# An attention-and-experts kernel: VectorE's transposes moved to the front of a unit, a shorter routing tail, other loads for two units, and steps of the seam moved

## The chip, the core and the metric

The kernel runs on one core of a Trainium2 chip. A core has five engines with instruction streams of their own: TensorE (PE in the rows, with its weight loads as PEld), VectorE (DVE), ScalarE (ACT), GpSimd (POOL) and SyncE (SP, which only starts DMAs here). Each engine works through its stream in order and waits on semaphores for the others. The metric is the device time of one execution in microseconds; lower is better.

## The reference

Two stages. First, attention for 4 batches of 12 heads, 448 positions, head size 64: scores are q times k over 8, softly capped as cap * tanh(scores / cap), then a softmax, then the product with v. Second, the result, seen as 1792 rows of 768, goes to a mixture of 8 experts: each row takes the expert with the greatest gate logit, and its output is `gate probability * sigmoid(output-gate logit of that expert) * (relu(x @ w1[e]) @ w2[e])`. All is float32.

```
scores = cap * tanh((q @ k.T / 8) / cap);  attn = softmax(scores);  x = attn @ v
e = argmax(x @ w_gate);  p = softmax(x @ w_gate)[e];  s = sigmoid(x @ w_output_gate)[e]
out = p * s * (relu(x @ w1[e]) @ w2[e])
```

## The kernel before

**Attention in 24 units.** A unit is a pair of heads of one batch (6 units to a batch). The loop `for u in range(NU)` (L958) writes each engine's stream by hand, and that order is final. In unit u, `qk(u, s)` (L353) makes four score tiles s = 0 to 3 on TensorE, and ScalarE takes the tanh of each (L371); `expo(u)` (L374) is one exponential over the unit; `pv(u - 1, c)` (L382) multiplies the unit before by V while that goes on; `u_evac(u - 1)` (L400) copies that product out of PSUM, on VectorE up to unit 7 and again for units 21 and 22, else on ScalarE. `presum` (L385) adds up the exponentials on GpSimd (on VectorE for the last units), and `sums` (L408) finishes the softmax denominators on TensorE. The exponentials of a unit lie in one of two buffers, so a unit's tanh may not write until `presum` of the unit two before has read that buffer.

**K and Q.** For float32 precision each K and Q is held as a rounded high plane and a low plane. Unit 0 is loaded in rows (`load_first`, L110) and transposed by TensorE (`prep_first`, L341). All other units are loaded by `load_pair` (L116) in pieces of 32 floats and transposed by VectorE: `t_k(u)` and `t_q(u)` (L307, L310) run a transpose into the PSUM tile `tk` (L286), a copy to the high plane (L276) and a subtraction to the low plane (L282). These turns wait in a list; `turn_next(n)` (L326) takes the next n of it, `before` of them right after the unit's score matmuls and `after` of them behind the matmuls with V. The pair is (1, 1) unless the table `TURN` says otherwise. There are five buffers of K and Q planes, and turns run up to some three units ahead.

**The ring of score tiles.** `scores()` and `half()` (L334, L338) hand out three PSUM tiles in turn: to the score tiles, to the product with V, and to every small step of the router. A tile is given again three requests later, and TensorE waits until its last reader is done with it.

**The router, in slots.** When a batch's units are done, `end_of_batch(b)` (L443) has its steps carried out in slots of the next batch's units: "f", "g" ahead of `expo`, "h" behind it, "q" behind the matmuls with V, "e" at the end. The dictionary `at` says which step goes where, counted from the first unit after the batch. The steps: `gate_mm` and `gate_out` (gate logits of four or two units in a score tile, copied out by VectorE as `gsb`), `sums_out`, `sums_tr`, `recips`, `gate_tr` and `gate_mul`, `logits`, `choose` (argmax), `rank_mm`, `place`, `place2` (each row's place in its expert's list), `enter` (the table entry: row number and weight), `scatter` (entries to the tables in DRAM, by GpSimd). `row_tr` and `row_out` write the attention rows to `xs` in DRAM; `store_rows` issues those stores on SP's queue.

**The seam.** During units 20 to 23 `early()` plans the first five blocks of rows in six pieces (`nx`); `set_known` opens the loads, `fetch_dma(i)` reads a block's table (SP), `gather(i)` its rows (POOL), `load_raw` brings the weights of the first expert (`lds`, 14 pieces, SP). Then the experts' matmuls begin: `split_to` (L1033) makes high and low planes of each weight piece (ScalarE L1044, VectorE L1045), `tx` transposes rows, and `mm_chunk` multiplies (L1066). The last batch's router runs in between, as steps of `bg`.

Of the kernel before, what the change touches and what calls it, by code (L numbers as in the profile page):

```python
# [22 lines left out]
def tile_kernel(ctx: ExitStack, tc, q, k, v, cap, w_gate, w_ogate, w1, w2, out):  # L23
# [35 lines left out]
    TURN = {5: (1, 2), 6: (1, 2), 8: (1, 2), 10: (2, 2), 14: (1, 2), 15: (1, 2), 16: (1, 2)}  # L59
# [40 lines left out]
    k0 = raw2[0][:, 0:SK + 128].rearrange("p (c j d) -> p c j d", j=2, d=D)  # L100
    q0 = raw2[1][0:CP, 0:NCH * 2 * D].rearrange("p (c j d) -> p c j d", j=2, d=D)
# [8 lines left out]
    def load_first():  # L110
        k_, q_ = heads(k, 0), heads(q, 0)
        load_natural(k0, k_, NK, 128, (nc.sync, nc.scalar))
        nc.scalar.dma_start(out=k0[0:64, NK], in_=k_[:, SK:S].rearrange("j p d -> p j d"))
        load_natural(q0, q_, NCH, CP, (nc.sync, nc.scalar))
# [38 lines left out]
    load_first()  # L153
# [36 lines left out]
    load_k(1)  # L190
    load_q(1)
# [35 lines left out]
    ids = rtp.tile([CP, B, NCH], F32, name="ids")  # L227
    nc.gpsimd.iota(ids, pattern=[[S, B], [CP, NCH]], base=-NT, channel_multiplier=1,
# [60 lines left out]
    def q_planes(u, ps):  # L289
        hi, lo = part_tile("QH", [128, S]), part_tile("QL", [128, S])  # L290
        copy(u == 0, hi, ps)
        minus(lo, ps, hi)
        return [hi, lo]

    def k_planes(u, ps):
        hi, lo = kpl[u % PB]
        parts = [(hi[:, 0:SK], lo[:, 0:SK], ps[:, 0:SK])]
        for j in range(2):
            h, c = slice(64 * j, 64 * j + 64), slice(SK + 64 * j, SK + 64 * j + 64)
            parts.append((hi[h, c], lo[h, c], ps[h, SK:S]))  # L300
        for x, _, y in parts:
            copy(u == 0, x, y)
        for x, z, y in parts:
            minus(z, y, x)
        return [hi, lo]

    def t_k(u):  # L307
        pl[u] = k_planes(u, turned(ldk.pop(u), S))

    def t_q(u):  # L310
        pl[u] += q_planes(u, turned(ldq.pop(u), S))

    loads = [f for u in range(2, NU, 2) for f in ((load_k, u), (load_q, u))]
    tdone = {t_k: 0, t_q: 0}

    def load_ahead():
        while loads:
            f, u = loads[0]
            if u > tdone[t_k if f is load_k else t_q] + 5:
# [4 lines left out]
    turns = [f for u in range(1, NU) for f in ((t_k, u), (t_q, u))]  # L324
# [16 lines left out]
    def prep_first():  # L341
        pk = tbank([128, S], "tk0")
        for c in range(NK + 1):
            n = min(128, S - c * 128)
            nc.tensor.transpose(pk[:, c * 128:c * 128 + n], k0[0:n, c].rearrange("p j d -> p (j d)"), ident[0:n, 0:n])
        pq = scores("tq0")[:, 0, 0:S]
        for c in range(NCH):
            nc.tensor.transpose(pq[:, c * CP:(c + 1) * CP], q0[:, c].rearrange("p j d -> p (j d)"), ident[0:CP, 0:CP])
# [994 lines left out]
```

## Time and profile before

| | us |
|---|---|
| median of 3 runs (537.25 to 537.8) | 537.76 |
| profiled execution, its own time | 541.76 |
| span in that profile | 540.2 |
| tanh of the first unit starts | 8.66 |
| exponentials of the last unit start | 217.27 |
| first expert matmul | 230.49 |
| mean granted clock of TensorE | 0.976 |

TensorE is busy for 498.9 us of the span (92%), VectorE 391.0 (72%), ScalarE 369.0 (68%), GpSimd 289.4 (54%). Attention takes the first 217 us or so, and the experts the rest. Times in rows are microseconds from the span's start; a share of busy time mixes the two stages, so each stage has to be read by itself.

### The profile page before, as it was taken

Reading aid. Unit: us, or ns where it says so; the run is one execution under the profiler, and the core shown is the slowest. Engines: PE = TensorE matmul, PEld = TensorE weight load, DVE = VectorE, ACT = ScalarE, POOL = GpSimd, SP = SyncE. Lnnn points to the kernel's source line nnn. Section 1 sums busy time; section 2 is a strip of 40 time slices with the busy share of each in tenths; the row PEclk is TensorE's granted clock in tenths of the full one; section 3 lists DMA queues with packets and bytes.
Section 4 is the critical chain, followed back from the end, with each engine's and each line's share of the span. In section 5 each row is a group of like instructions: output and inputs, shape, how many; then the busy total and the mean of one; then the engine's idle time right before and its main releaser. Section 6 shows DMA issues by size and latency. Waiting matters only on the chain. (4 is left out here: it accounts for less than half of the span.)

```text
span 540.2 us, 10059 instructions
## 1 busy us (share of the span) xinstructions
PE 498.9 (92%) x3077; PEld 345.0 (64%) x3077; DVE 391.0 (72%) x713; ACT 369.0 (68%) x427; POOL 289.4 (54%) x360
## 2 busy tenths in 40 slices
PE   7699989959994989899999999999999999999994
PEld 5344355424452445267898997897879877666691
DVE  4578789987998666379898996894757685546450
ACT  5789877838874576554758896885766786555551
POOL 8999887776887530335625877214647035262001
PEclk9999999979998899989999999999999999999999
DMA  7978755843522043798319924419939969993001
GB/s 128 179 147 144 124 98 96 154 85 70 101 55 51 18 78 60 248 343 246 116 42 388 361 69 147 183 42 366 364 109 370 333 201 385 335 353 137 0 32 47
DMA packets 155932, 91.93 MB, mean 170 GB/s; under 512 B 138578, under 2 KB 138714, under 8 KB 155872
## 3 DMA queue, kind: packets, MB, share of 16 engines
q1 hardware_dynamic: 144000, 57.78, 40.6%
q0 software_dynamic: 8832, 32.74, 16.6%
q10 hardware_dynamic: 3040, 0.71, 0.6%
q8 instruction: 26, 0.43, 0.3%
q14 instruction: 34, 0.28, 0.2%
HBM read 123.68 MB, written 12.04 MB: 251 GB/s over the span
## 5 line engine op out<-in xcount | busy, mean ns | idle before, releaser
L1045 DVE TENSOR_TENSOR wr<-raw,wr 128x768 fp32r<-128x768 f32 (+1 forms) x167 | 172.1, 1067 | 70.6 <-ACT wr L1044 62.2
L1044 ACT ACTIVATE wr<-raw 128x768 fp32r<-128x768 f32 (+1 forms) x167 | 150.2, 935 | 38.4 <-DMA raw<-in_moe_w_dram 17.9
L371 ACT ACTIVATE pt<-s,icap 128x896 f32<-128x896 f32 x96 | 80.8, 914 | 40.8 <-PE s L364 28.0
L382 PE MATMUL u<-pt,vv 128*64 128x448 f32 x384 | 80.5, 563 | 1.3 <-ACT pt L371 0.8
L1066 PE MATMUL py<-wr,hh 128*128 128x384 f32 x352 | 77.3, 340 | 0.0
L1066 PE MATMUL php<-wr,xh 128*128 128x512 f32 x264 | 75.6, 408 | 0.0
L1135 POOL DMA_INDIRECT out_dram<-yo,ti x13 | 20.5, 1575 | 94.8 <-ACT yo L1133 70.6
L374 ACT ACTIVATE pt<-pt,capc 128x3136 f32<-128x3136 f32 x24 | 69.9, 2912 | 0.6
L1066 PEld LDWEIGHTS py<-wr,hh 128*128 128x128 f32 x352 | 61.2, 188 | 4.0 <-issue 3.7
L393 POOL TENSOR_TENSOR pa<-pt 128x896 f32<-128x896 f32 x20 | 42.1, 2106 | 25.9 <-ACT pt L374 19.4
L1066 PEld LDWEIGHTS php<-wr,xh 128*128 128x128 f32 x264 | 48.0, 190 | 12.2 <-issue 1.8
L382 PEld LDWEIGHTS u<-pt,vv 128*64 128x64 f32 x384 | 26.3, 142 | 43.5 <-issue 36.5
L398 POOL TENSOR_TENSOR pb<-pb,pt 64x448 f32<-64x448 f32 x40 | 45.6, 1141 | 3.1
L1066 PE MATMUL py<-wr,hl 128*128 128x384 f32 x176 | 44.8, 335 | 0.0
L394 POOL TENSOR_TENSOR pb<-pa,pt 128x896 f32<-128x896 f32 x20 | 42.2, 2111 | 1.6
L1066 PE MATMUL php<-wr,xl 128*128 128x512 f32 x132 | 41.9, 398 | 0.0
L1182 POOL DMA_DIRECT2D rh<-in_moe_w_dram x42 | 23.2, 556 | 21.9 <-DVE wr L1045 13.6
L286 DVE STREAM_TRANSPOSE tk<-raw 128x448 f32<-128x448 f32 x46 | 30.1, 655 | 4.9 <-issue 4.0
L1066 PEld LDWEIGHTS py<-wr,hl 128*128 128x128 f32 x176 | 31.8, 188 | 0.0
L1066 PEld LDWEIGHTS php<-wr,xl 128*128 128x128 f32 x132 | 25.0, 190 | 6.2
L1236 POOL DMA_INDIRECT out_dram<-yh,toh x6 | 6.2, 1039 | 32.0 <-issue 8.7
L853 POOL DMA_INDIRECT xg<-xs,ti x14 | 17.2, 1229 | 10.6 <-PE pt_x L865 4.7
(324 smaller groups left out, 833.7 us busy)
## 6 DMA issues: line engine op xcount, KB each, us to landing
raw<-in_moe_w_dram SPq DMA_DIRECT2D x78, 512.0 KB
raw<-in_moe_w_dram SPq DMA_DIRECT2D x104, 384.0 KB
rh<-in_moe_w_dram POOLq DMA_DIRECT2D x18, 512.0 KB
rh<-in_moe_w_dram POOLq DMA_DIRECT2D x24, 384.0 KB
raw<-in_q_dram SPq DMA_DIRECT2D x45, 112.0 KB
raw<-in_k_dram SPq DMA_DIRECT2D x44, 112.0 KB
vv<-in_v_dram SPq DMA_DIRECT2D x44, 96.0 KB
xs<-xr SPq DMA_DIRECT2D x36, 112.0 KB
```

Of the source, the lines that this page charges most:

```text
L286: nc.vector.transpose(out=ps, in_=src.rearrange("p r a -> p (r a)"))
L371: nc.scalar.activation(out=pt[u][:, 2 * s:2 * s + n], in_=ps, func=ACTF.Tanh, scale=icap)
L374: nc.scalar.activation(out=pt[u], in_=pt[u], func=ACTF.Exp, scale=capc)
L382: nc.tensor.matmul(ups[u][64 * j:64 * j + 64], lhsT=V[:, c, j, :], rhs=P[:, 2 * c + (j if c < NK else 0)], start=(c == 0), stop=(c == NK))
L393: eng.tensor_tensor(out=a, in0=P[:, 0:2], in1=P[:, 2:4], op=ALU.add)
L394: eng.tensor_tensor(out=s1[u], in0=a, in1=P[:, 4:6], op=ALU.add)
L398: eng.tensor_tensor(out=s1[u][h, j], in0=s1[u][h, j], in1=P[h, 2 * NK], op=ALU.add)
L1044: nc.scalar.activation(out=t[:, 0, 0:F], in_=raw, func=ACTF.Copy)
L1045: nc.vector.tensor_tensor(out=t[:, 1, 0:F], in0=raw, in1=t[:, 0, 0:F].bitcast(F32), op=ALU.subtract)
L1066: nc.tensor.matmul(ps[g][:, 0:n], lhsT=st[:, c], rhs=w[:, z, g * n:(g + 1) * n], start=(c == 0 and st is hi and z == 0), stop=(c == (KD, K ...
L1135: nc.gpsimd.indirect_dma_start(out=out, out_offset=bass.IndirectOffsetOnAxis(ap=ti, axis=0), in_=y, in_offset=None, bounds_check=NT - 1, o ...
L1182: nc.gpsimd.dma_start(out=d, in_=rows_of(src, e, w, c), **kw)
```

## The change

- `TURN` is written anew and its default becomes (2, 0): both turns come ahead of a unit's slots; where a unit has a third or fourth turn, `turn_next(after)` now comes behind `u_evac`.
- `place2` and `enter` lose instructions: the place is reduced straight into the integer tile, the row number is written once at the start into a table `ent` for all batches, one `scalar_tensor_tensor` replaces two instructions.
- Units 1 and 2 are loaded in rows as unit 0 is, on SP's queue, followed by V of units 0 and 1 (which ScalarE's queue issued before), and are transposed by TensorE in units 0 and 1. VectorE's turns begin with unit 3.
- `gate_mm` and `gate_out` of the first four units of a batch move from slot (-1, "q") to (-2, "q"): units 5, 11 and 17 instead of 6, 12 and 18.
- In the seam `early()` runs five pieces at the end of unit 20 instead of three, `fetch_dma` of blocks 0 and 1 and the first weight loads come in unit 21 ahead of the last row stores, two more weight loads come ahead of `fetch_dma` of blocks 2 and 3; `presum` also runs for unit 22, so the last `sums` has fewer matmuls; `split_to(SP0)` comes behind the last `u_evac`.

```diff
-    TURN = {5: (1, 2), 6: (1, 2), 8: (1, 2), 10: (2, 2), 14: (1, 2), 15: (1, 2), 16: (1, 2)}
+    TURN = {0: (0, 0), 1: (0, 0), 5: (2, 1), 6: (2, 1), 8: (2, 1), 10: (2, 2), 14: (2, 1), 15: (2, 1), 16: (2, 1)}
...
-    load_k(1)
-    load_q(1)
+    for u in range(1, NN):
+        load_nat(u, (nc.sync, nc.sync))
+    load_v(0)
...
+    def first_planes(pk, pq):
+        k_, (main, *tails) = k_parts(0, pk)
+        q_, (q0,) = q_parts(0, pq)
+        copy(True, main[0], main[2])
+        copy(True, q0[0], q0[2])
+        for x, _, y in tails:
+            copy(False, x, y)
+        for x, z, y in (main, q0, *tails):
+            minus(z, y, x)
+        return k_ + q_
...
-    loads = [f for u in range(2, NU, 2) for f in ((load_k, u), (load_q, u))]
+    loads = [f for u in (NN, *range(NN + 1, NU, 2)) for f in ((load_k, u), (load_q, u))]
...
     def presum(u, s):
-        if u >= NU - 2:
+        if u >= NU - 1:
...
-                for g in range(4):
+                for g in (range(4) if c == 0 else (2, 3)):
...
         def place2():
             rk = rt["rk"]
             nc.vector.tensor_tensor(out=rk, in0=rk, in1=rt["ohb"], op=ALU.mult)
-            p_ = T("pos", [CP, NCH])
-            nc.vector.tensor_reduce(out=p_, in_=rk, axis=AX.X, op=ALU.add)
-            nc.vector.tensor_copy(out=T("posi", [CP, NCH], U32), in_=p_)
+            nc.vector.tensor_reduce(out=T("posi", [CP, NCH], U32), in_=rk, axis=AX.X, op=ALU.max)
...
             nc.vector.tensor_reduce(out=den[:, 0], in_=rt["ex"], axis=AX.X, op=ALU.add)
-            nc.vector.tensor_scalar(out=den[:, 0], in0=den[:, 0], scalar1=1e-9, scalar2=None, op0=ALU.add)
             nc.vector.tensor_scalar(out=den[:, 1], in0=den[:, 1], scalar1=1.0, scalar2=None, op0=ALU.add)
-            nc.vector.reciprocal(out=den, in_=den)
-            ent = T("ent", [CP, NCH, 2])
-            nc.vector.tensor_copy(out=ent[:, :, 0], in_=ids[:, b])
-            nc.vector.tensor_tensor(out=ent[:, :, 1], in0=den[:, 0], in1=den[:, 1], op=ALU.mult)
+            stt(den[:, 0], den[:, 0], 1e-9, ALU.add, den[:, 1], ALU.mult)
+            nc.vector.reciprocal(out=ent[:, b, :, 1], in_=den[:, 0])
...
-            at = {(-1, "q"): [g0], (0, "q"): [g1], (0, "e"): [sums_out], (1, "g"): [t[1]],
+            at = {(-2, "q"): [g0], (0, "q"): [g1], (0, "e"): [sums_out], (1, "g"): [t[1]],
...
-            at = {(-1, "q"): [g0], (0, "f"): [P(sums, EARLY), g1, sums_out], (0, "h"): [t[1], *gts, logits, choose],
-                  (1, "g"): [rank_mm, place, rws[0]], (1, "h"): [place2, enter, scatter], (1, "q"): [rws[1]],
-                  (1, "e"): [nx] * 3,
-                  (2, "g"): [rws[2], rws[3]], (2, "h"): [nx], (2, "q"): [rws[4], rws[5]], (2, "e"): [*[nx] * 2, P(set_known, NE)],
-                  (3, "f"): [fd[0], fd[1], *lds[:2]],
-                  (3, "h"): [P(gather, 0), P(gather, 1)], (3, "e"): [fd[2], fd[3], *lds[2:KD]], (4, "f"): lds[KD:]}
+            at = {(-2, "q"): [g0], (0, "f"): [P(sums, EARLY), g1, sums_out], (0, "h"): [t[1], *gts, logits, choose],
+                  (1, "g"): [rws[0], rank_mm, place], (1, "h"): [place2, enter, scatter], (1, "q"): [rws[1]],
+                  (1, "e"): [nx] * 5,
+                  (2, "g"): [rws[2], rws[3]], (2, "h"): [nx, P(set_known, NE), store_rows],
+                  (2, "q"): [fd[0], fd[1], rws[4], rws[5], store_rows, *lds[:2]],
+                  (3, "h"): [P(gather, 0), P(gather, 1), *lds[2:4]], (3, "e"): [fd[2], fd[3], *lds[4:KD]], (4, "f"): lds[KD:]}
...
         for s in range(NK):
             qk(u, s)
-        load_ahead()
+            if u == 0 and s == 0:
+                pl[1] = planes_of(k_parts(1, nat_k(1)))
+            if u == 0 and s == 1:
+                pl[1] += planes_of(q_parts(1, nat_q(1)))
+        if u > 0:
+            load_ahead()
         qk(u, NK)
-        before, after = TURN.get(u, (1, 1))
+        if u == 1:
+            pl[2] = planes_of(k_parts(2, nat_k(2)))
+            pl[2] += planes_of(q_parts(2, nat_q(2)))
+        before, after = TURN.get(u, (2, 0))
         turn_next(before)
...
-        turn_next(after)
         if u > 1 and u - 2 != EARLY:
             sums(u - 2)
         slot(u, "q")
         if u > 0:
             u_evac(u - 1)
+        turn_next(after)
...
-    split_to(SP0)
     bg.extend(end_of_batch(B - 1))
     pv(u, NK)
     u_evac(u)
+    split_to(SP0)
     sums(u)
```

## Rows read from the trace of the kernel before

**Rows 1.** Busy time by stretch: sum, per engine (instructions), granted clock, DMA share, GB/s.
```profile
109.00:127.00 18.00, 11.71 (x71) 6.12 (x65) 13.79 (x28) 7.82 (x9) 12.98 (x10) 0.81 0.58 105
176.00:178.00 2.00, 2.00 (x9) 1.03 (x11) 0.00 (x0) 1.20 (x2) 1.65 (x2) 0.50 0.02 1
270.00:280.00 10.00, 10.00 (x60) 10.00 (x59) 9.52 (x34) 5.15 (x6) 0.00 (x0) 1.00 0.03 2
```

**Rows 2.** Waits of TensorE, 0 to 225 us: total, times, longest.
```profile
PE s L364 <- DVE gsb L276: 11.6, 2, 6.3
...
PE s L364 <- DVE ut L405: 3.1, 3, 1.3
```

**Rows 3.** Timeline, units 12 and 13: start, length, engine, line, [idle before <- what ended it].
```profile
102.26 0.36 PE L364 MATMUL s<-QH,K2H 64*128 64x448 f32 x2
102.28 0.19 DVE L524 TENSOR_REDUCE den<-og 112x4 f32<-112x32 f32 x1
...
108.39 2.11 POOL L393 TENSOR_TENSOR pa<-pt 128x896 f32<-128x896 f32 x1 [1.74 <-ACT pt L374]
...
108.51 0.96 PE L478 MATMUL tg<-ut,wg 128*32 128x448 f32 x8
...
108.70 1.83 DVE L550 CAST posi<-pos 112x4 uint32<-112x4 f32 x1
...
110.65 2.03 DVE L556 TENSOR_SCALAR den<-den 112x4 f32<-112x4 f32 x1
...
112.91 0.98 DVE L560 COPY ent<-ids 112x4 f32<-112x4 f32 x1
...
116.50 0.62 DVE L276 COPY gsb<-tg 128x448 f32<-128x448 f32 x1
...
117.17 0.74 PE L364 MATMUL s<-QH,K3H 64*128 64x448 f32 x2 [6.29 <-DVE gsb L276]
```

**Rows 4.** VectorE's groups by shape, 45 to 180 us: busy, mean ns of one, idle before.
```profile
L286 DVE STREAM_TRANSPOSE tk<-raw 128x448 f32<-128x448 f32 x36 | 23.6, 655 | 0.7
L276 DVE CAST QH<-tk 128x448 fp32r<-128x448 f32 x18 | 11.2, 624 | 0.6
...
L276 DVE CAST K2H<-tk 128x384 fp32r<-128x384 f32 x4 | 2.2, 558 | 0.2
...
L276 DVE CAST K3H<-tk 64x64 fp32r<-64x64 f32 x8 | 1.7, 217 | 0.1
```

**Rows 5.** Timeline, units 13 to 19.
```profile
126.05 0.62 DVE L276 COPY gsb<-tg 64x448 f32<-64x448 f32 x1 [1.88 <-PE tg L478]
...
161.29 0.19 DVE L524 TENSOR_REDUCE den<-og 112x4 f32<-112x32 f32 x1
...
174.20 0.61 DVE L276 COPY gsb<-tg 128x448 f32<-128x448 f32 x1
...
174.87 0.74 PE L364 MATMUL s<-QH,K4H 64*128 64x448 f32 x2 [5.30 <-DVE gsb L276]
```

**Rows 6.** Timeline, units 0 to 2.
```profile
17.85 2.09 POOL L393 TENSOR_TENSOR pa<-pt 128x896 f32<-128x896 f32 x1
...
24.58 3.33 ACT L371 ACTIVATE pt<-s,icap 128x896 f32<-128x896 f32 x4 [3.48 <-POOL pb L398]
```

**Rows 7.** Timeline, the seam.
```profile
220.42 0.69 DVE L942 CAST wr<-raw 128x1024 fp32r<-128x1024 f32 x1 [6.81 <-DMA raw<-in_moe_w_dram]
...
223.39 2.46 PE L420 MATMUL sm<-pt,ohc 128*32 128x448 f32 x24
...
223.84 16.00 SPq L815 DMA_DIRECT2D raw<-in_moe_w_dram  x18
...
227.69 1.06 ACT L1044 ACTIVATE wr<-raw 128x1024 fp32r<-128x1024 f32 x1 [3.81 <-DMA raw<-in_moe_w_dram]
228.66 0.53 ACT L403 ACTIVATE ut<-u 128x448 f32<-128x448 f32 x1
...
230.49 1.91 PE L1066 MATMUL php<-wr,xh 128*128 128x512 f32 x4
```

More of the change, by code (lines that the diff above doesn't have):

```diff
@@ L99, in tile_kernel @@
     SK = NK * 128
-    k0 = raw2[0][:, 0:SK + 128].rearrange("p (c j d) -> p c j d", j=2, d=D)
-    q0 = raw2[1][0:CP, 0:NCH * 2 * D].rearrange("p (c j d) -> p c j d", j=2, d=D)
+    NN = 3
+    nat = [[raw2[2 * u][:, 0:SK + 128].rearrange("p (c j d) -> p c j d", j=2, d=D),
+            raw2[2 * u + 1][0:CP, 0:NCH * 2 * D].rearrange("p (c j d) -> p c j d", j=2, d=D)] for u in range(NN)]
     vvs = [ldp.tile([128, 2, NK + 1, 2, D], F32, name=f"vv{i}", bufs=1) for i in range(2)]
@@ L108, in load_natural, with load_nat @@
             engs[j].dma_start(out=dst[:, 0:n, j], in_=src[j, 0:n * m].rearrange("(c p) d -> p c d", c=n))
[L110 to L114, printed above, removed]
+    def load_nat(u, engs):
+        (k0, q0), k_, q_ = nat[u], heads(k, u), heads(q, u)
+        load_natural(k0, k_, NK, 128, engs)
+        engs[1].dma_start(out=k0[0:64, NK], in_=k_[:, SK:S].rearrange("j p d -> p j d"))
+        load_natural(q0, q_, NCH, CP, engs)
     def load_pair(src, u, base, to):
@@ L152, in tile_kernel @@
     nc.vector.memset(wz, 0.0)
-    load_first()
+    load_nat(0, (nc.sync, nc.scalar))
     nc.scalar.dma_start(out=capc, in_=cap.to_broadcast([128, 1]))
@@ L322, in load_ahead @@
             loads.pop(0)
-    turns = [f for u in range(1, NU) for f in ((t_k, u), (t_q, u))]
+    turns = [f for u in range(NN, NU) for f in ((t_k, u), (t_q, u))]
     def turn_next(n):
@@ L339, in half, with nat_k @@
         return scores(name)[:, 0]
-    def prep_first():
+    def nat_k(u):
         pk = tbank([128, S], "tk0")
@@ L417, in sums @@
             for c in range(NK + 1):
-                for g in range(4):
+                for g in (range(4) if c == 0 else (2, 3)):
                     j = g % 2
-                    nc.tensor.matmul(smt[b][32 * g:32 * g + 32], lhsT=ohc[:, r, :] if c < NK else ohl[:, j],
-                                     rhs=pt[u - 1 + g // 2][:, 2 * c + (j if c < NK else 0)], start=False, stop=(c == NK))
+                    d = g > 1
+                    nc.tensor.matmul(smt[b][32 * g:32 * g + 32], lhsT=ohl[:, j] if d and c == NK else ohc[:, r, :],
+                                     rhs=pt[u][:, 2 * c + (j if c < NK else 0)] if d else s1[u - 1][:, j],
+                                     start=False, stop=(c == NK or not d))
             return
@@ L954, in tile_kernel @@
     warm(WARM[1])
-    load_ahead()
+    load_ahead(NN + 1)
     slots.setdefault((2, "f"), []).append(eps)
     for u in range(NU):
-        if u > 2 and u % 2:
+        if u % 2:
             load_v(u + 1)
```

50 lines of the change are left out of this document (24 added, 26 removed).

## The prediction, made before the changed kernel was run

> **What bounds the kernel now.** I read the busy times by stretch first, then what TensorE waited for, then the timeline around its longest waits. In the expert stage TensorE is busy without a gap at the full clock (10.00 of 10 us at 270 [rows 1]), so whatever attention saves is carried to the end and nothing done to VectorE there counts. In the attention stage no engine is full, and the time is lost in a few places. The largest is one form of wait: TensorE's third score tile waits for VectorE to copy the gate logits (`gsb`) out of the same ring tile, 11.6 us in 2 waits [rows 2]. Both are in the unit in which the batch before also has `place2` and `enter`. In the first [rows 3] the gate matmuls run at 108.51, but VectorE's stream still holds the rest of `place2` and `enter` and a K turn, so the copy starts at 116.50 and TensorE stands for 6.29 us. In the second [rows 5] the copy starts at 174.20 and the wait is 5.30. After each, TensorE works at the lower of its two levels (1.2 of 2.4 GHz; granted 0.50 at 176 to 178, 0.81 over 109 to 127 [rows 1]). A third form, 3.1 us in 3 waits [rows 2], is a copy of the product with V behind a turn on VectorE. At the start the bound is another: unit 2's tanh begins at 24.58 when GpSimd's `presum` of unit 0 is done, and that began at 17.85 [rows 6], because GpSimd's set-up ran until then.
>
> **Units 11 to 13.** A K turn on VectorE is 655 + 558 + 2 x 217 for the transpose and the copies and as much again without the transpose for the subtractions (their rows have the same means): 2.64 us. A Q turn is 655 + 2 x 624 ns = 1.90 [rows 4]. With (2, 0) unit 11 has its second turn, a K, ahead of its slots. `choose` ended at 102.28 + 0.19 = 102.47 [rows 3]; now at 105.11, and the gate copy, which moves to this unit, ends 0.62 later, at 105.73. TensorE wants the third tile of unit 12 at 102.26 plus the 0.96 of the gate matmuls [rows 3], 103.22: it waits 2.5 us. Unit 12 then has no gate. From third tile to third tile the trace has 102.26 to 117.17 - 6.29 = 110.88, that is 8.62, or 7.66 without the gate. So unit 13's third tile comes at 113.39 instead of 117.17: 3.8 us won. VectorE must by then have done two turns (4.54) and `place` and one row copy (1.6 by the same steps in unit 12 before): 105.73 + 6.1 = 111.9, just when unit 13's first tiles ask for those ring tiles (a gap of about 1.1 us before the third): no wait, but no slack.
>
> **The shorter entries.** The cast (1.83), one of two scalar additions and the copy (0.98) go from this stretch, and a product becomes one instruction with the addition [rows 3]. The cast is as long as it is because it stands until GpSimd's instruction of 108.39 + 2.11 is over; the other addition (2.03) and the copy show the same beside the next GpSimd instructions. Without them 3.05 us go from VectorE's chain in unit 12, but since the gate no longer stands behind it I count nothing for it besides; its bounds are 0 and 3.05 twice, 6.1. The Trainium skill's page "SBUF — State Buffer", section "Who interferes with whom", says that a VectorE instruction with two SBUF inputs, or a scalar addition in a two-port mode, is shut out while GpSimd holds the shared port, and that reductions never are. The row of the cast agrees. By that rule the new fused instruction and the addition that stays could each wait a whole GpSimd instruction, the saving would fall from 3.05 to about 0.9 us a batch, and the time would be up to 2 us above my sum.
>
> **Units 13 to 19.** About 3.7 us of TensorE's work after the first wait ran at half clock; at full clock half of it, 1.8, comes back (bounds 0, if the shorter wait also drops the clock, and 1.8). So the next gate copy, at 126.05 [rows 5], 8.88 after the old third tile, comes 7.1 after the new one, at 120.5: 5.5 us ahead. From about 129 to 174 VectorE runs without a pause, so its own work sets the rest. `choose` in unit 17 ended at 161.29 + 0.19 = 161.48 [rows 5]; less 5.5, plus the Q turn now ahead of it (1.90), 157.9; with the copy, moved here too, 158.5. That is the third tile of unit 18, TensorE having waited some 3 us. Unit 19's follows 7.66 later, at 166.2 against 174.87 [rows 5]: 8.7. The half clock behind the second wait [rows 1] gives another 1.8: 10.5. Against this I set 1.5 us for tiles that now ask for a row copy or `place` standing behind the second turn (units 11, 12 and 18 have no slack). The three waits behind `ut` [rows 2] go, but in units 5 to 7 the third turn and the gate copy now stand ahead of that copy in turn, so I count 0 (bounds -1 and +3.1). **Attention: 9.0 us.** Bounds: 15, if neither new wait appears, and the slower case below.
>
> **The start.** Loading units 1 and 2 in rows, and V from SP, brings planes sooner but not unit 2's tanh, which GpSimd's set-up and `presum` hold [rows 6], and neither changes. TensorE gets two sets of transposes (about 1.7 us each) in unit 0 and 1; unit 1's end moves up to 1.1 us because Q's transpose takes a ring tile, hidden by the 3.48 us in which ScalarE waits anyway. GpSimd then goes from one `presum` to the next with 0.7 us of idle time up to unit 6, so at most that is won: 0, bounds -1.0 and +0.7.
>
> **The seam.** Before, ScalarE stands for weight piece 2 (3.81 us, until 227.69), and the last copy of the product with V, in the stream behind it, comes at 228.66; the first expert matmul at 230.49 [rows 7]. Now that copy is ahead of the splits. Weight loads: SP's stores (about 1.1 us each) and the table fetches (4.9 for two blocks) stay ahead of the first two pieces, so these come only about 1.5 us sooner, but pieces 2 and 3 no longer stand behind the next two fetches (they were issued from 223.84 [rows 7]) and land before 223. The rounding of the first piece, 220.42 [rows 7], moves to 218.9; with its low plane (1.2) and the new `presum` of unit 22 (3.4 us on VectorE, the length that unit 20's has) VectorE is ready at 224.3. The last `sums` waits for that about 1 us longer than now, but has 20 of 32 matmuls: the 24 at 223.39 took 2.46 [rows 7] and eight more 0.9, so 2.1 instead of 3.4, to 226.4. Transposes (1.0) and the gate (0.96) follow: first expert matmul at 228.4, 2.1 sooner. If the clock does not fall at 231 to 234 as it did, up to 2 us more. I take 3.0; bounds 0 (VectorE later by the new `presum`) and 4.5. Moving `nx` and `set_known` costs nothing: VectorE idles some 2 us in unit 21 at that place.
>
> **Sum.** 9.0 + 0 + 3.0 = 12.0 from the profiled execution's 541.76 (span 540.2 and 1.6 around it): 529.8. It lies 4.0 above the median of the runs shown, 537.76; the same 12.0 off that gives **525.8**.
>
> **Rivals.** *The wait moves and does not shrink.* The gate copy stands in unit 11 and 17 behind `choose`, which also has instructions that wait for GpSimd, and VectorE is full there; for it speaks the row of 161.29, against it that the copy no longer has `enter` ahead. Then only the 3.05 us a batch stay, about 3 in all on the path, and the seam's 3: 531.8. *The seam gives nothing*, since the new `presum` holds `sums`: 528.8. *GpSimd becomes the bound*: 6.6 us of `presum` a unit and 5 us of `scatter` in units 13 and 19 are close to a unit's 7.7; if that takes back 5 us: 530.8. *Slower: turns first is paid in every unit whose slot "g" has a VectorE step.* These are units 9 to 13 and 15 to 18, nine; if VectorE is behind when such a unit's scores begin (in unit 12 it was: its first turn could not begin before 102.47, the scores began near 101), the turn put ahead, 2.27 us on the mean, delays the ring tile for TensorE by all of it: 20.4 us lost. Won are the two waits (11.6), about 3.6 of clock and the seam's 3, together 18: 537.76 + 2.4 = 540.2. It decides once VectorE's backlog at a unit's start is over some 1 us in most of these; against it speaks the ledger above, in which it is so in three.
>
> **Chances.** Forecast 0.52 (own range 521 to 530); moved wait 0.17; no gain in the seam 0.10; GpSimd 0.05; slower 0.12; gains and losses even, near 537, 0.04. Faster by over 0.2% (1.1 us, about what a measurement of this kernel can tell from no change): 0.84; within it 0.04; slower 0.12. The range 520 to 534 leaves out the last two cases and little of the others' edges.
>
> **What would show it.** Right: no wait of TensorE on `gsb` over 3 us, and none in unit 13 or 19; the granted clock near 1.00 at 109 to 127 and 168 to 186 of the old places; unit 2's tanh still at 24.5 behind GpSimd; first expert matmul near 218. Wrong: waits of 2 us on `xr` or `pre` copies in each row unit (slower case), a `gsb` wait of 5 us in units 12 and 18 (moved), or GpSimd's `pb` ending ScalarE's waits in units 14 to 20.

## The result, and the profile after

The changed kernel takes 530.12 us (median of 4 executions, 529.38 to 531.11) against 537.78 (537.25 to 540.07) for the kernel before on the same chip: ratio 0.9851, 95% interval 0.9817 to 0.9885. That is faster by 7.7 us and lies inside the forecast range of 520 to 534, 4.3 above the forecast of 525.8.

| us | before | after |
|---|---|---|
| median beside each other | 537.78 | 530.12 |
| profiled execution, its own time | 541.76 | 529.38 |
| span in that profile | 540.2 | 527.6 |
| exponentials of unit 13 / 16 / 19 / 23 start | 120.78 / 145.73 / 180.01 / 217.27 | 117.41 / 145.69 / 173.47 / 208.83 |
| first expert matmul | 230.49 | 219.79 |
| first expert matmul to the end of the span | 309.7 | 307.8 |

The profiled execution of before is the slowest of those shown and the one of after the fastest of its four, so the two traces differ by 12.4 us and the medians by 7.7.

First the busy time by stretch, in the kernel after. The columns are those of [rows 1]: the stretch, its sum, busy time (instructions) of PE, PEld, DVE, ACT, POOL, then TensorE's granted clock, DMA share and GB/s.

```profile
109.00:127.00 18.00, 17.20 (x109) 8.56 (x108) 16.15 (x42) 15.87 (x18) 12.54 (x9) 1.00 0.70 105
130.00:140.00 10.00, 7.21 (x35) 3.34 (x31) 8.40 (x20) 6.24 (x5) 9.06 (x7) 0.83 0.71 135
168.00:186.00 18.00, 17.36 (x112) 9.35 (x110) 13.75 (x40) 13.67 (x16) 15.98 (x12) 1.00 0.32 65
270.00:280.00 10.00, 10.00 (x56) 8.80 (x55) 9.44 (x10) 8.07 (x11) 6.41 (x11) 1.00 0.95 363
```

Where before TensorE had 11.71 of 18 us busy at a clock of 0.81 [rows 1], it now has 17.20 at 1.00. But a new hole is at 130 to 140 (7.21 of 10, clock 0.83). The same three stages of both kernels, from the exponentials of unit 10 to those of 13, 16 and 19, show the exchange; before:

```profile
88.93:120.78 31.85, 24.56 (x148) 12.87 (x147) 28.69 (x63) 20.67 (x20) 24.74 (x18) 0.90 0.58 103
120.78:145.73 24.95, 24.39 (x151) 12.26 (x150) 20.92 (x48) 20.79 (x20) 18.26 (x11) 0.99 0.49 92
145.73:180.01 34.28, 26.24 (x156) 12.56 (x155) 27.50 (x60) 21.11 (x21) 24.59 (x18) 0.90 0.20 42
```

and after:

```profile
88.24:117.41 29.17, 25.14 (x152) 13.04 (x153) 27.83 (x63) 20.68 (x20) 18.31 (x12) 0.94 0.59 106
117.41:145.69 28.28, 25.20 (x150) 12.45 (x146) 23.31 (x54) 20.68 (x20) 25.21 (x18) 0.94 0.65 105
145.69:173.47 27.78, 25.43 (x157) 12.84 (x157) 24.75 (x52) 20.96 (x21) 18.45 (x12) 0.94 0.21 43
```

The first stage is 2.7 us shorter, the second 3.3 longer, the third 6.5 shorter. At unit 16 this execution stands exactly where before stood; all that attention gains in it comes behind that unit. Next, what TensorE waited for, and then ScalarE, up to 225 us (total, times, longest); these answer to [rows 2]:

```profile
PE s L390 <- ACT pt L392: 6.6, 3, 2.5
PE tg L501 <- DVE xr L599: 3.1, 1, 3.1
PE s L385 <- DVE gsb L278: 2.0, 1, 2.0
PE s L385 <- DVE ut L426: 1.9, 3, 0.8
...
PE s L385 <- DVE xr L599: 1.5, 3, 0.9
...
ACT pt L392 <- POOL pb L419: 5.7, 2, 2.9
```

The wait on `gsb` fell from 11.6 us in two to 2.0 in one. Two others appeared. The gate matmuls (`tg`) wait 3.1 us for a row copy, and ScalarE waits for `pb`, the end of GpSimd's `presum` (one of the two waits in that row is the old one of unit 2, now 2.90; the other is new). The timeline around the first, in units 11 and 12:

```profile
102.67 1.29 DVE L599 TENSOR_TENSOR xr<-trow,rec 112x512 f32<-112x512 f32 x2
103.41 0.96 PE L501 MATMUL tg<-ut,wg 128*32 128x448 f32 x8 [3.10 <-DVE xr L599]
...
106.27 0.61 DVE L278 COPY gsb<-tg 128x448 f32<-128x448 f32 x1
...
112.95 2.12 POOL L414 TENSOR_TENSOR pa<-pt 128x896 f32<-128x896 f32 x1 [7.09 <-ACT pt L395]
...
113.22 1.88 DVE L577 TENSOR_SCALAR den<-den 112x4 f32<-112x4 f32 x1
115.13 0.17 DVE L662 SCALAR_TENSOR_TENSOR den<-den 112x4 f32<-112x4 f32 x1
115.15 2.13 POOL L415 TENSOR_TENSOR pb<-pa,pt 128x896 f32<-128x896 f32 x1
115.33 0.18 DVE L579 RECIPROCAL ent<-den 112x4 f32<-112x4 f32 x1
```

The gate copy starts at 106.27 instead of 116.50 [rows 3], and `enter` at 113 no longer stands ahead of it. But the gate matmuls need a tile of the ring, the one given to unit 11's first row tile, and VectorE's copy of that row stands behind both turns of unit 11. GpSimd's row of 112.95 shows what the late unit did to it: it had stood idle for 7.09 us until unit 12's exponentials, which start at 109.90. The second new wait, in units 13 to 15:

```profile
120.01 1.12 POOL L585 DMA_INDIRECT tab<-ent,posi  x1 [0.30 <-POOL pb L419]
...
123.97 0.96 POOL L585 DMA_INDIRECT tab<-ent,posi  x1 [0.30 <-issue]
...
125.00 2.09 POOL L414 TENSOR_TENSOR pa<-pt 128x896 f32<-128x896 f32 x1
...
131.06 1.13 POOL L419 TENSOR_TENSOR pb<-pb,pt 64x448 f32<-64x448 f32 x1 [0.56 <-DMA tab<-ent,posi]
132.22 3.33 ACT L392 ACTIVATE pt<-s,icap 128x896 f32<-128x896 f32 x4 [2.85 <-POOL pb L419]
...
133.28 0.47 PE L390 MATMUL s<-QH,K0H 128*128 128x448 f32 x1 [2.50 <-ACT pt L392]
```

GpSimd issues the four table scatters from 120.01 to 124.93, begins unit 13's `presum` only then, and unit 15's tanh, which writes the buffer that this reads, starts 2.85 us late; TensorE stops for 2.50, and the granted clock behind it gives the 0.83 above. The start and the seam, which answer to [rows 6] and [rows 7]:

```profile
17.86 2.10 POOL L414 TENSOR_TENSOR pa<-pt 128x896 f32<-128x896 f32 x1
...
24.61 3.33 ACT L392 ACTIVATE pt<-s,icap 128x896 f32<-128x896 f32 x4 [2.90 <-POOL pb L419]
...
209.26 0.69 DVE L959 CAST wr<-raw 128x1024 fp32r<-128x1024 f32 x1 [3.97 <-DMA raw<-in_moe_w_dram]
...
215.06 0.54 ACT L424 ACTIVATE ut<-u 128x448 f32<-128x448 f32 x1 [3.33 <-PE u L403]
215.51 1.99 ACT L1063 ACTIVATE wr<-raw 128x1024 fp32r<-128x1024 f32 x2
...
219.79 1.19 PE L1085 MATMUL php<-wr,xh 128*128 128x512 f32 x4
```

In the start, GpSimd's first `presum` and unit 2's tanh have not moved by more than 0.03 us. In the seam the last copy of the product with V (215.06) is now ahead of the splits (215.51), ScalarE waits for no weight piece, and from the last exponentials to the first expert matmul it takes 10.96 us instead of 13.22; in a second execution of the change it is 12.26, with the reason shown under "The seam" below.

### The profile page after: what moved, and what is told of

Read it like the earlier page. It is cut to its first block, busy times and chain, and to the rows that moved or that the text cites. A ratio compares the mean times of both kernels' runs of the same rounds, so it can differ in the third digit from the quotient of the medians.

```text
span 527.6 us, 10057 instructions
## 1 busy us (share of the span) xinstructions
PE 498.7 (95%) x3081; PEld 345.6 (66%) x3081; DVE 386.4 (73%) x703; ACT 369.2 (70%) x425; POOL 292.5 (55%) x360
## 5 line engine op out<-in xcount | busy, mean ns | idle before, releaser
L1154 POOL DMA_INDIRECT out_dram<-yo,ti x13 | 18.6, 1433 | 84.5 <-ACT yo L1152 61.0
L288 DVE STREAM_TRANSPOSE tk<-raw 128x448 f32<-128x448 f32 x42 | 27.5, 656 | 0.9
```

Source lines behind the costliest of these rows:

```text
L288: nc.vector.transpose(out=ps, in_=src.rearrange("p r a -> p (r a)"))
L1154: nc.gpsimd.indirect_dma_start(out=out, out_offset=bass.IndirectOffsetOnAxis(ap=ti, axis=0), in_=y, in_offset=None, bounds_check=NT - 1, o ...
```

## The experiments

The kernel before ran beside each of them; its median was 541.42 us (536.87 to 543.93) in the first group, 541.45 in the second, 537.52 in the third and 539.14 in the fourth. The changed kernel gave 530.12 beside a before of 537.78 and 529.27 beside one of 541.42: in these two groups its own time moved by 0.9 us, that of before by 3.6. On these two alone rests the choice made here, to compare kernels by their own times, with 1 us either way as an estimate; where the ratios to before would say something else, that is given too. Diffs are against the changed kernel.

**First group: the change again, and three parts of it.** `e0_change_again` is the changed kernel unchanged.

> The changed kernel as it is, for comparison on the same chip as the next three. 529 to 531.5 us. Theory: TensorE waits for xr and gsb in units 11, 12, 17 and 18 (about 5 and 2 us), ScalarE waits about 2.9 us for GpSimd's pb in unit 15.

Measured: 529.27 us (527.14 to 530.5), ratio 0.9785, interval 0.9741 to 0.9829. Its trace has the stage 13 to 16 at 26.33 us, 2 shorter than the trace above, with a wait on GpSimd of 1.16 in unit 15. What follows: that stall is in both traces of the change, but its length varies. The wait of the gate matmuls on `xr` is 3.09, as in the trace above; on `gsb` it is 3.2 in two, in units 12 and 18.

`e1_gates_back` puts the gates back by a unit. (In `at`, 0 stands for the second unit after the batch, 7, 13 or 19, so -2 is unit 5, 11 or 17.)

```diff
-            at = {(-2, "q"): [g0], (0, "q"): [g1], (0, "e"): [sums_out], (1, "g"): [t[1]],
+            at = {(-1, "q"): [g0], (0, "q"): [g1], (0, "e"): [sums_out], (1, "g"): [t[1]],
```

> The gate matmuls and their copy go back one unit, all else as in the change. Theory (the gain in attention is that the copy no longer stands behind place2 and enter): waits on gsb of 4 to 5.5 us return in units 13 and 19, the wait of the gate matmuls on xr in unit 11 (3.1 us) goes; 533 to 535 us. Rival (the order of turns and the shorter entries make the gain, the gate's unit is indifferent): no gsb wait over 2.5 us, 529 to 531.

Measured: 529.38 us (527.67 to 531.59), ratio 0.9791 (0.9746 to 0.9836), the same as the change; `gsb` 4.3 us in 2 waits. My first theory, that the move of the gates is what gains, fell here by the time. I had also expected the `xr` wait to go. It did not: it is 3.11 us, now ahead of unit 12's first scores, so it does not need the gate. The equal time hides gains and losses. With the gates back, unit 6's exponentials come at 55.30 instead of 57.01, the stage 10 to 13 takes 31.86 us instead of 29.17, and the stage 13 to 16 takes 24.99 instead of 28.28 (26.33 in `e0_change_again`), with no wait on GpSimd in unit 15. So the move does save 2.7 us between units 10 and 13, and pays for it ahead of unit 6 and behind unit 13.

`e2_turns_back` puts the turns back to one ahead and one behind, and the copies of the product with V behind the turn.

```diff
-    TURN = {0: (0, 0), 1: (0, 0), 5: (2, 1), 6: (2, 1), 8: (2, 1), 10: (2, 2), 14: (2, 1), 15: (2, 1), 16: (2, 1)}
+    TURN = {0: (0, 0), 1: (0, 0), 5: (1, 2), 6: (1, 2), 8: (1, 2), 10: (2, 2), 14: (1, 2), 15: (1, 2), 16: (1, 2)}
...
-        before, after = TURN.get(u, (2, 0))
+        before, after = TURN.get(u, (1, 1))
...
+        turn_next(after)
         if u > 1 and u - 2 != EARLY:
...
-        turn_next(after)
```

> Turns as before: one ahead of a unit's slots and one behind the matmuls with V (two behind in units 5, 6, 8, 14, 15, 16), gates still a unit sooner. Theory (the order of turns is worth little, since VectorE is full and serves the same work): 529 to 532, the wait on xr in unit 11 shrinks from 3.1 to under 1, the wait on gsb in unit 12 grows by 2 to 3. Rival (turns first is a good part of the gain): 533 or more, with waits behind ut of 3 us in units 6 to 9.

Measured: 530.73 us (528.24 to 533.36), ratio 0.9827 (0.9782 to 0.9872); 1.5 above the change, less than the runs tell apart. The 3.1 us wait of the gate matmuls on `xr` is gone, and `gsb` waits 6.5 us in 2 in its place (2.52 and 4.01). Neither part alone, then, holds the gain.

`e3_scatter_later` issues the table scatter one unit later in batches 0 and 1.

```diff
-                  (5, "g"): [rank_mm, place, rws[4]], (5, "h"): [place2, enter], (6, "g"): [scatter, rws[5]]}
+                  (5, "g"): [rank_mm, place, rws[4]], (5, "h"): [place2, enter], (6, "g"): [rws[5]], (7, "g"): [scatter]}
```

> GpSimd's scatter of the first two batches comes one unit later (units 14 and 20), behind presum of unit 13 and 19. Theory (part of my sum was taken back by GpSimd: the scatter of 5 us stands ahead of presum, and tanh of unit 15 waits for it): ScalarE's wait on pb in unit 15 (2.85 us) and the half clock after it go; 526 to 528.5. Rival (GpSimd is full, the wait only comes a unit later): 529.5 to 531.

Measured: 533.47 us (530.43 to 535.26), ratio 0.9858 (0.9811 to 0.9905), slower than the change by 4. The wait in unit 15 went (stage 13 to 16: 25.52 us), but the scatter of batch 1 now comes in unit 20, where batch 2 writes its own places into the same tile. VectorE, and then TensorE in its trace:

```profile
191.37 0.18 DVE L571 TENSOR_REDUCE posi<-rk 112x4 uint32<-112x32 f32 x1 [6.80 <-DMA tab<-ent,posi]
...
192.81 0.74 PE L385 MATMUL s<-QH,K1H 64*128 64x448 f32 x2 [4.62 <-DVE bcnt L655]
```

`place2` waits 6.80 us until the transfers that read `posi` have landed, and the stage 19 to 23 takes 40.70 us instead of 36. The time lies above both ranges expected: they had not seen this second reader.

**Second group: one part each again.** `e4_units_11_17` gives units 11 and 17 one turn ahead and one behind.

```diff
-    TURN = {0: (0, 0), 1: (0, 0), 5: (2, 1), 6: (2, 1), 8: (2, 1), 10: (2, 2), 14: (2, 1), 15: (2, 1), 16: (2, 1)}
+    TURN = {0: (0, 0), 1: (0, 0), 5: (2, 1), 6: (2, 1), 8: (2, 1), 10: (2, 2), 11: (1, 1), 14: (2, 1), 15: (2, 1), 16: (2, 1), 17: (1, 1)}
```

> The change, but in units 11 and 17 only one turn stands ahead of the slots and the other behind (1, 1). Theory (the second turn ahead of the slots is what made the row copies late and TensorE wait in these units): the gate matmuls' wait on xr in unit 11 falls from 3.1 to under 1 us, the waits on gsb from 2.0 to under 1; 527 to 529 us. Rival (VectorE is full, the same wait appears at place and xr of units 12 and 18): 529.5 to 531.

Measured: 527.96 us (526.94 to 529.52), ratio 0.976 (0.9732 to 0.9788). The gate matmuls' wait on `xr` fell to 0.3, `gsb` waits 3.6 in 2 (under 1 was expected), and TensorE waits 2.9 in 2 for `rk`. In all TensorE waits for VectorE about as long, in shorter pieces, and the clock from 88 to 121 is 1.00 instead of 0.95. Unit 12's exponentials start at 107.02 instead of 109.90, and ScalarE does not wait for GpSimd in unit 15, although unit 14 comes at about the same time (126.33 and 126.03).

`e5_entries_back` takes the shorter entries back.

```diff
-            nc.vector.tensor_reduce(out=T("posi", [CP, NCH], U32), in_=rk, axis=AX.X, op=ALU.max)
+            p_ = T("pos", [CP, NCH])
+            nc.vector.tensor_reduce(out=p_, in_=rk, axis=AX.X, op=ALU.add)
+            nc.vector.tensor_copy(out=T("posi", [CP, NCH], U32), in_=p_)
...
```

> place2 and enter with their former instructions (cast, addition, product and copy back), all else as in the change. Theory (no one waits for the end of enter any more except the scatter): VectorE has 1 to 4 us more in units 12 and 18, the time is 0 to 2 us above the change: 530 to 532. Rival (VectorE is the bound and pays in full): 3 us a batch, 534 to 536.

Measured: 531.58 us (530.23 to 533.23), ratio 0.9819 (0.9791 to 0.9847): some 2 us worse than the change (1.5 against 530.12, 2.3 against 529.27). The forecast had counted nothing for this part. TensorE in unit 14 of its trace shows one place where the longer entries are paid:

```profile
124.54 0.74 PE L385 MATMUL s<-QH,K4H 64*128 64x448 f32 x2 [3.32 <-DVE xr L605]
```

The row copy that it waits for stands behind the longer entries and two turns on VectorE; in the two traces of the change this wait is absent or 1.32 us.

`e6_loads_back` loads units 1 and 2 as before.

```diff
-    NN = 3
+    NN = 1
...
-    for u in range(1, NN):
-        load_nat(u, (nc.sync, nc.sync))
-    load_v(0)
+    load_k(1)
+    load_q(1)
...
```

> Units 1 and 2 loaded in pieces of 32 floats and turned by VectorE again, V of units 0 and 1 from ScalarE's queue. Theory (GpSimd's set-up and presum hold unit 2): unit 2's tanh stays at 24.5 to 24.7, 529 to 531 us, no difference over 0.7. Rival (the natural loads spare DMA time and VectorE in units 2 to 5): 531.5 to 534.

Measured: 526.87 us (526.81 to 530.12), ratio 0.9749 (0.972 to 0.9777), the lowest median of all. The natural loads gain nothing. Whether they cost up to 2 us is not settled: at unit 13 the two traces stand 0.2 us apart (117.19 and 117.41), and at unit 16 2.4 us (143.32 and 145.69), because the stall on GpSimd in unit 15 varies (0.97 here); `e0_change_again`, with 1.16, has unit 16 at 143.65.

`e7_seam_back` puts back the seam's steps, the last `sums` and the place of the splits.

```diff
-        if u >= NU - 1:
+        if u >= NU - 2:
...
+    split_to(SP0)
     bg.extend(end_of_batch(B - 1))
     pv(u, NK)
     u_evac(u)
-    split_to(SP0)
...
```

> The seam as before (early plan, fetches, weight loads, last sums, order of the first splits), the gates still a unit sooner. Theory: the distance from the last unit's exponentials to the first expert matmul goes from about 11.0 back to about 13.2 us and the clock falls at the start of the experts; 532 to 534.5 us. Rival (hidden by DMA or by the expert stage's own waits): 529.5 to 531.

Measured: 531.85 us (529.91 to 534.14), ratio 0.9829 (0.9798 to 0.9859), 1.7 to 2.6 above the change. From the exponentials of unit 23 to the first expert matmul it takes 13.84 us.

Undone one at a time, the gates, the turns, the entries, the loads and the seam cost 0.1, 1.5, 2, -2.8 and 2 us, 3 in all, of the 7.7 to 12 that they gain together. So some of them stand in for one another. The third and fourth groups ask which.

**Third group: two parts at once, and a lighter unit 10.** `f1_gates_turns_back` has the edits of `e1_gates_back` and `e2_turns_back` together.

> The changed kernel with two parts undone together: the gate matmuls and the gate copy in unit 12 and 18 again instead of 11 and 17, and one turn ahead of a row unit's slots and one behind, with the copy of the product with V ahead of the turn that follows it. Entries, natural loads and seam as changed. Theory that the two parts are substitutes (undone alone, the one cost 0 and the other 1.5 us, since either keeps the gate copy from standing behind place2, enter and a turn): together they cost most of the attention gain. The gsb waits come back in unit 13 and 19 with 3 to 6 us each (less than before's 6.3 and 5.3 by the shorter entries), and the time is 533 to 537, 4 to 8 above the changed kernel. Rival, the parts are independent: the costs add, 1.5 us, 530 to 531, and the gsb waits stay under 3 us; then the gain is from neither.

Measured: 532.74 us (530.92 to 535.36), ratio 0.9898 (0.9863 to 0.9933), 2.6 to 3.5 above the change, just under the range of the first theory and above that of the rival. The trace decides more than the time. TensorE in units 13 and 19:

```profile
115.51 0.74 PE L385 MATMUL s<-QH,K3H 64*128 64x448 f32 x2 [4.17 <-DVE gsb L278]
...
171.93 0.74 PE L385 MATMUL s<-QH,K4H 64*128 64x448 f32 x2 [4.01 <-DVE gsb L278]
```

Both long waits are back in their old places, 4.17 and 4.01 us instead of 6.29 and 5.30 [rows 3, 5]. Undone alone gates and turns cost 0.1 and 1.5, together about 3 by the kernels' own times (2.5 to 6 by the ratios to before, 0.9898 against 0.9851 and 0.9785). By the times that is not far from adding up, within what these runs tell apart; in the waits on `gsb` (2.0 and 3.2 us in the two traces of the change, 4.3 and 6.5 with one undone, 8.2 with both) the turns carry most of it.

`f2_unit10_two_turns` moves two of unit 10's four turns to units 7 and 9.

```diff
-    TURN = {0: (0, 0), 1: (0, 0), 5: (2, 1), 6: (2, 1), 8: (2, 1), 10: (2, 2), 14: (2, 1), 15: (2, 1), 16: (2, 1)}
+    TURN = {0: (0, 0), 1: (0, 0), 5: (2, 1), 6: (2, 1), 7: (2, 1), 8: (2, 1), 9: (2, 1), 14: (2, 1), 15: (2, 1), 16: (2, 1)}
```

> The changed kernel with only the spread of turns changed: unit 10, which does four (two ahead of its slots, two behind), does two, and units 7 and 9, which do two, do three each; the same turns in all. Theory that VectorE's fullness in units 10 to 12 sets the wait at unit 12 (xr, 3.1 us): VectorE reaches unit 11's row steps some 4 us earlier, the xr wait falls below 1 us, the half clock behind it goes, and the time is 526 to 528 (2 to 3 below the changed kernel), unless units 7 and 9 now wait for planes' ring tiles, which would show as waits on pre copies there. Rival, the wait is the order within unit 11 and not the load: xr wait stays near 3 us and the time within 1 us of the changed kernel. Second rival, the gain is given back at unit 15, where GpSimd's scatter holds presum: stage of units 10 to 13 shorter by 3 us, stage 13 to 16 longer by as much, time the same.

Measured: 528.37 us (524.49 to 530.71), ratio 0.9798 (0.9757 to 0.9839). The wait of the gate matmuls on `xr` is gone with the order within unit 11 as in the change: a lighter unit 10 removes it as another order does (`e2_turns_back`, `e4_units_11_17`). But the stage 6 to 10 became 0.8 us longer (32.01), the stage 10 to 13 only 1.2 shorter (28.01), the `gsb` waits are 1.78 and 3.02, the stage 16 to 19 takes 29.97 us instead of 27.78, and ScalarE waits 2.22 for GpSimd in unit 15. The time is 0.9 to 1.8 below the change with a spread of 6, so a gain isn't shown. The second rival, that unit 15 takes back what is won, is not shown either: the stage 13 to 16, 27.50 us, lies between those of the two traces of the change.

**Fourth group: all of attention undone, and the best edits together.** `f4_attention_back` has the edits of `f1_gates_turns_back` and `e5_entries_back`; the seam and the loads stay as changed.

> The changed kernel with the three attention parts undone together: gates again in unit 12 and 18, turns one ahead and one behind, and the longer table entries (casts, second addition, copy). What stays of the change are the seam steps and the natural loads of units 1 and 2. If the parts' costs add (gates and turns together 3 us as just run, entries 2.3), 535 to 536. Theory that the entries cost more when the gate copy stands behind them (they lie between place2 and that copy, up to 3.05 us in each of two batches): the gsb waits in unit 13 and 19 are again 5 to 6 us each as in the kernel before, and the time is 536.5 to 539, within some 3 us of the kernel before, the seam's share. Rival: the kernel before has lost time elsewhere too, which the loads gave back; then it stays at or below 535 and the rest to the kernel before, over 3 us, is the loads'.

Measured: 536.46 us (534.77 to 540.83), ratio 0.9945 (0.9917 to 0.9972), 2.7 below the kernel before beside it. Unit 12 to 13 in its trace, to be set beside [rows 3]:

```profile
108.61 1.83 DVE L573 CAST posi<-pos 112x4 uint32<-112x4 f32 x1
...
110.56 2.04 DVE L579 TENSOR_SCALAR den<-den 112x4 f32<-112x4 f32 x1
112.51 0.16 DVE L580 TENSOR_SCALAR den<-den 112x4 f32<-112x4 f32 x1
...
112.82 0.98 DVE L583 COPY ent<-ids 112x4 f32<-112x4 f32 x1
...
116.41 0.62 DVE L278 COPY gsb<-tg 128x448 f32<-128x448 f32 x1
...
117.09 0.74 PE L385 MATMUL s<-QH,K3H 64*128 64x448 f32 x2 [6.29 <-DVE gsb L278]
```

The old stall is back to the hundredth, 6.29 us at 117.09 (before: 117.17). The second, in unit 19, is 3.78 us instead of 5.30, with a wait of 2.75 instead of 1.80 for `rk` ahead of it. The step from `f1_gates_turns_back` to this kernel is the entries alone, and it costs 3.7 us (2.5 by the ratios; 2.1 of it in this one wait), against 2 when the gates and turns are as changed. Undone together the three parts cost 6.4 us (536.46 less 530.1) to 7.2 (less 529.3), by the ratios 5 to 8.6; one by one, 0.1 + 1.5 + 2.

`f3_best` joins the edits of `e4_units_11_17` and `e6_loads_back` and a later scatter for batch 0 alone.

```diff
-                  (5, "g"): [rank_mm, place, rws[4]], (5, "h"): [place2, enter], (6, "g"): [scatter, rws[5]]}
+                  (5, "g"): [rank_mm, place, rws[4]], (5, "h"): [place2, enter], (6, "g"): [rws[5]] if b == 0 else [scatter, rws[5]]}
+            if b == 0:
+                at[(7, "g")] = [scatter]
```

> The changed kernel with three of the edits that ran better or removed a wait: units 1 and 2 loaded as before the change, units 11 and 17 one turn ahead and one behind, and GpSimd's scatter of the first batch alone a unit later. If they add to the changed kernel's 530 what they gave alone (loads -2.4, turns -1.7, scatter 0 to -2 by the wait of 2.9 on GpSimd in unit 15 with its half clock), 524 to 526. Rival: they meet in the same stretch, units 13 to 16, and only the largest counts: 526.5 to 528. In both, no wait of ScalarE on GpSimd's pb over 1 us and none of TensorE on xr over 1 us in units 12 to 16.

Measured: 528.09 us (526.06 to 528.94), ratio 0.9785 (0.9752 to 0.9819), no better than `e6_loads_back` or `e4_units_11_17` alone. ScalarE:

```profile
139.59 3.33 ACT L391 ACTIVATE pt<-s,icap 128x896 f32<-128x896 f32 x4 [2.38 <-POOL pb L418]
...
193.43 1.01 ACT L391 ACTIVATE pt<-s,icap 128x896 f32<-128x896 f32 x1 [2.46 <-DVE pb L418]
```

The scatter was moved by one unit, and a stall of 2.38 us stands in unit 16, where both expectations had none over 1. Four scatters take 4.9 us of GpSimd and a `presum` 6.6, together 11.5 in a unit of some 7.7. A stall need not follow, though: `e3_scatter_later`, with the same move and unit 15's exponentials 1.3 us later (134.59 against 133.29), has none in unit 16. And at unit 19, which this execution reaches 4.9 us earlier than the one above (168.59 against 173.47), 4.2 us are lost until unit 23 (39.52 us for the stage instead of 35.36), with the wait of 2.46 on VectorE's `presum` above and a granted clock of 0.91 in that stage. The wait alone does not do it: `e2_turns_back` has the same one, 2.47 us, at a clock of 1.00, and takes 35.66 us there. Why the clock fell in one and not in the other is open. My expectation of 524 to 526 failed, and the rival, whose range ends 0.1 us under the time measured, is the nearer one.

## Why the prediction was right, and where it was not

**What bound the kernel.** Right. With the three attention parts undone, the wait of 6.29 us comes back unchanged, with the same instructions ahead of the copy; with them, in both traces of the change, no `gsb` wait is over 3 us and none lies in unit 13 or 19. The other signs of being right came too: a granted clock of 1.00 at 109 to 127 and at 168 to 186 in both. One sign of being wrong came as well, `pb` ending a wait of ScalarE in unit 15.

**Units 11 to 13 and 13 to 19: a size and a missed wait.** The term for attention was 9.0 us. The runs give 6.4 to 7.2 (the three parts undone). In the profiled execution it was 3.4 us by unit 13 (forecast 3.8), 0.0 by unit 16, 6.5 by unit 19 (forecast 8.7 for its third tile) and 8.4 by unit 23. Two things were missed.

- In "TensorE wants the third tile of unit 12 at 103.22: it waits 2.5 us" I asked only when the copy comes, not whether the gate matmuls get their ring tile. They waited 3.10 for the row copy of the same unit before they began. Against such waits the sum had 1.5 us, for all units; this one alone took twice that. The third tile came not much later than forecast for it (the copy ended at 106.88, forecast 105.73), but the wait is in a place where the clock fell behind it.
- I had set "GpSimd becomes the bound" at 0.05, as a rival of its own and of 5 us. It came as a part of the forecast case: unit 12's `presum`, `scatter` and unit 13's `presum` follow each other without a gap, and unit 15 pays 2.85 us and the half clock in the execution profiled, 0.97 to 2.22 in four others (`e0_change_again`, `e6_loads_back`, `e7_seam_back`, `f2_unit10_two_turns`).

The two belong together, which I had overlooked. GpSimd has time to spare ahead of it (18.31 of 29.17 us busy from unit 10 to 13); it begins unit 12's `presum` only when that unit's exponentials are done, and the late gate matmuls make that unit late. In the five traces with the stall, unit 12's exponentials start at 108.60 or later. In the six with the scatter in its place that start them at 107.29 or earlier (before, `e1_gates_back`, `e2_turns_back`, `e4_units_11_17`, `f1_gates_turns_back`, `f4_attention_back`) there is none, though `e4_units_11_17` is about as early as the change at unit 14. (`e5_entries_back` starts them at 109.37 without a stall, but its unit 14 is 3.6 us later than in the change.) No run delays unit 12 alone, so this is read from the traces and not proved. Nor is it shown that the two make up all of the 1.8 to 2.6 us that are missing: `e4_units_11_17`, with a wait of 0.3 and no stall, is 1.3 to 2.2 us below the change.

**The credit was put to the wrong part.** The text gave the gain to the gates' move, with turns ahead of the slots as what pays for it. The runs show that the gates' move gains nothing in the whole (0.1, with 2.7 us won between units 10 and 13 and lost elsewhere), that the turns' order is worth some 1.5, about what the runs tell apart, and both together 3; the rest of attention's 6.4 came with the entries, 3.7 in that order. VectorE has 27.83 of 29.17 us busy from unit 10 to 13 in the changed kernel; what I had not drawn from its fullness is that an order then mostly chooses which of its results is late.

**The shorter entries.** Counted 0, bounds 0 and 6.1; measured about 2 with the rest of the change, 3.7 without gates and turns. To count nothing "since the gate no longer stands behind it" was wrong in a stretch where VectorE is full: the row copies stand behind it too, and with the longer entries TensorE waits 3.32 us for one of them. The length itself was right. From the reduction of the places to the end of the entry, VectorE takes 2.54 us in unit 12 of `f1_gates_turns_back` (109.66 to 112.20) and 5.47 in that of `f4_attention_back` (108.39 to 113.86); the difference is 2.93, forecast 3.05.

The row of 113.22 has the addition waiting, 1.88 us for four elements a partition, until GpSimd's instruction of 112.95 is over; the fused instruction right behind it took 0.17. The Trainium skill, page "SBUF — State Buffer", section "Who interferes with whom", has such an instruction blocked for the whole of a GpSimd instruction that holds the shared port, and the trace agrees for the first. That the second would wait too, which would have left 0.9 us of the saving, it did not show. (The prediction also has the time up to 2 us above its sum in that case; but the sum counts nothing for the entries, so a smaller saving could not have raised it.)

**The start.** Right in the sum: 0 was forecast, tanh of unit 2 stayed at 24.6 in the trace above, and undoing the loads lost nothing. The reason does not hold in every execution: in `e0_change_again` that tanh starts at 25.77 and waits 4.04 us for TensorE's scores, not for GpSimd. By unit 3's exponentials nothing of this is left (35.29 against 35.55 before).

**The seam.** Right in kind, somewhat too large. Forecast 3.0 (0 to 4.5), 2.1 of it ahead of the first expert matmul: that comes 2.3 us sooner behind the last exponentials in the first trace of the change and 1.0 in the second. `f4_attention_back` against before gives 2.7 us (1.5 to 4.5 by its interval), with the loads in it, and undoing the seam alone 1.7 to 2.6. The clock did not fall behind the first expert matmul: it is 1.00 at 220 to 224, while before it was 0.50 at 231 to 234. What holds that matmul in the second trace is the first weight piece. VectorE rounds it when it has landed, then does unit 22's `presum`, and the last `sums` waits for that:

```profile
209.76 0.69 DVE L959 CAST wr<-raw 128x1024 fp32r<-128x1024 f32 x1 [5.46 <-DMA raw<-in_moe_w_dram]
...
214.62 1.22 PE L442 MATMUL sm<-pb,ohc 128*32 128x448 f32 x3 [0.58 <-DVE pb L419]
...
220.11 1.20 PE L1085 MATMUL php<-wr,xh 128*128 128x512 f32 x4
```

In all twelve traces with the changed seam the first expert matmul comes, within 0.1 us, at the later of two times: 10.96 us behind unit 23's exponentials, or some 10.34 behind the start of this rounding; in eight of them it is the second. So "whatever attention saves is carried to the end" holds only as long as the weights come in time. `e4_units_11_17` starts the exponentials of unit 23 3.4 us sooner than the trace above (205.45 against 208.83) and its first expert matmul only 2.0 (217.81 against 219.79).

**From the trace to the median.** The sum was 12.0 from the profiled execution's 541.76, so 529.8, and the profiled execution of after has 529.38. That this is so close is in part luck: the one was the slowest of its kernel, the other the fastest. The same 12.0 was then taken off the median, 537.76. Whether the faster executions of before have as much to save is not shown, since only one of them has a trace, and they differ by up to 7 us on one chip. By medians the gain is 7.7 there and 12.15 in the first group. The forecast of 525.8 is 4.3 too low: 1.8 to 2.6 of it are attention's, up to 1.3 the seam's, and for the rest there is this step and the spread of the executions.

**The rivals.** The slower case, with turns first paid in every row unit, happened in one unit (the 3.10 us), not in nine, and it took both unit 10's four turns and the two ahead in unit 11: without the one (`f2_unit10_two_turns`) or the other (`e4_units_11_17`) the wait is 0 or 0.3 us. The moved wait did not come in its form: `gsb` waits 2.0 and 3.2 in all in the two traces of the change.

## What to carry to other kernels

When a wait ends on an engine that is 95% busy in that stretch, moving the awaited step, reordering what stands ahead of it and shortening that can stand in for one another: here the three cost 3.6 us undone one at a time and 6.4 to 7.2 together. So undo them together as well before you credit one of them, and price an instruction saved on that engine between nothing and its own length (here 2.9 us in each of two batches, worth 2 to 3.7 in all). When a step is moved earlier, ask what it needs itself, the buffer it writes first of all, before asking when its reader gets it. For an engine off the path, look at when its work may begin, and not only at how much there is: GpSimd had stood idle for 7 us before the burst that held up unit 15. And ask what else the next stage waits for: a saving in attention reached the experts only where the first weight piece was there.

## What the runs showed of the hardware

- A `TENSOR_SCALAR` of 112x4 elements took 0.16 us with GpSimd idle (`e2_turns_back`, 108.81), and 1.78 to 2.10 in the traces where it stood beside a GpSimd addition of 128x896; a small one right behind a delayed one took 0.16 to 0.17, although GpSimd's next instruction began within 0.15 us of it (115.13 and 115.15 above).
- A tile that an indirect DMA reads its positions from is not free when GpSimd has issued it: in `e3_scatter_later` the last of four issues ended at 187.70, and VectorE could write `posi` at 191.37.
- The executions of one kernel on one chip differ by 2.6 to 7.1 us in the groups of five or more (before: 536.87 to 543.93), while five of the six of `e6_loads_back` lie within 0.2 us.
